# Attention and a SiLU projection pair on one core: q, k and v loaded over all 128 partitions in one transfer, attention output on four quarter-array tiles

## The chip, the cores and the metric

The kernel runs on one core of a Trainium2 chip. The metric is the device time of one execution in microseconds (us), on the slowest core, which here is the only one. Each kernel was executed several times. "Fast" and "slow" are the states that the runs were given by their time and clock. The profile is one execution, traced. In it PE is TensorE's matmuls, PEld its weight loads, DVE is VectorE, ACT ScalarE, POOL GpSimd and SP SyncE, which issues most transfers.

## The reference

Linear attention over 8 batches, 8 heads, 576 tokens and 64 features per head, then a two-layer projection with SiLU on the 4608 tokens.

```python
q_s = exp(q) / sum(exp(q), over features)          # max subtraction left out here
k_s = exp(k) / sum(exp(k), over the sequence)
kv  = einsum('bhsd,bhse->bhde', k_s, v)            # 64 x 64 per head
x   = einsum('bhsd,bhde->bhse', q_s, kv)           # heads side by side: [4608, 512]
h   = x @ w_in                                     # [4608, 2048]
out = (h * sigmoid(h)) @ w_out                     # [4608, 512]
```

## The kernel before

Tokens lie on partitions: of the 128 partitions, 64 hold the tokens of one head (nine tokens, `J`, per partition) and 64 those of another. The 4608 tokens go through the projections in nine chunks: mm1 (`hps`, 16 groups of 4 matmuls per chunk), tanh on ACT and a product on DVE (`GT`), mm2 (`ops`, 16 groups of 4). Attention for batch b is planned a chunk ahead, between those groups: exp of q and k on ACT, normalization on DVE and POOL, a transposing transfer of q (`qT`), `kv` on PE, and `xt`, which multiplies `qT` by kv into `XT`, the input of mm1.

The loads. One tensor of one batch comes in four transfers of 288 KB, and each fills 64 partitions:

```python
def load(b, name, src, ccs=(0, 1), engs=(nc.sync, nc.sync)):
    ...
    x = src[b].rearrange("(c r g) (p j) d -> c r p g (j d)", r=2, g=2, j=J)
    for cc in ccs:
        for r in range(2):
            engs[r].dma_start(
                out=st[b][name][r * P:(r + 1) * P, 2 * cc:2 * cc + 2, :], in_=x[cc, r])
```

kv and xt. kv comes out per half `r` and pair `g`; it is copied into a block-diagonal 128x128 weight `kvbd` (zeroed once), so that one full-array matmul serves two heads:

```python
nc.vector.tensor_scalar_mul(                       # in kvcopy, for r, for g
    out=kvbd[b % 3][h, 2 * cc + r, g * 64:(g + 1) * 64],
    in0=kp[h, g * E1:g * E1 + D], scalar1=rz[h, g:g + 1])
...
nc.tensor.matmul(                                  # in xt(t, c), c = 0..3
    out=o1[:, a - first:a - first + n],
    lhsT=kvbd[b % 3][:, c, :],
    rhs=st[b]["qT"][:, col // P:(col + n) // P, cc, r * P:(r + 1) * P])
```

The start. Batch 0's loads go first, q and the first part of k from two issuing engines (SP and ACT), the rest from SP. The weights (`W1`, `W2`, fp32 in memory and cast to bf16 on the way) are issued by POOL once the first half of v is there. Batch 1's loads wait for a part of W2:

```python
nc.gpsimd.tensor_copy(gate[:, 0:1], st[0]["vt"][0:1, 1, 0:1])
load_w1(0); load_w1(1); load_w2(0); load_w1(2); load_w2(1); load_w1(3); load_w2(2); load_w2(3)
st[1]["qt"] = ld.tile(...)
nc.gpsimd.tensor_copy(st[1]["qt"][0:1, 0, 0:1], W2[0:1, 4, 0:1])   # gate of batch 1
for name, src in (("qt", q), ("kt", k), ("vt", v)):
    load(1, name, src)
```

## Time and profile before

| what | before |
|---|---|
| median of the first 3 runs | 316.25 us (316.21 to 318.23) |
| the traced run | 312.93 us, span 311.2 us |
| PE busy | 286.4 us, 92% of the span |
| steady chunk (512 tokens) | 30.43 us |
| first projection matmul starts | 21.90 us |

The page's view in 40 equal slices (7.8 us each) of the kernel before. Digits are busy tenths, PEclk is the granted clock in tenths, the last row is what the DMA engines moved.

```profile
PE   8559985889689999999999999999999999999992
...
PEclk9979999899979999999999999999999999999998
DMA  7999999999999898289838974500450050014005
GB/s 179 259 208 207 246 250 256 236 271 278 258 242 254 185 251 199 65 177 238 189 85 177 243 166 100 112 2 0 101 113 0 2 126 10 0 36 102 0 0 135
```

Read it from left to right and count the slices from 0: up to slice 11 the DMA engines are full (9, but for the first slice) and PE falls to 5 or 6 in four slices. From slice 12 PE is full, and the load of the DMA engines sinks, to 2 in slice 16 and to 0 in slice 26. The kernel has a DMA-bound stage and a TensorE-bound stage, and the average of 92% hides the first.

The chain of work that ended last, of the kernel before, as shares of the span:

```profile
PE 65%; DMA 24%; DVE 5%; POOL 1%; ACT 1%; SPq 1%; issue 1%; DVEq 0%
PE ops L231 32%; PE hps L196 30%; DMA vt<-in_v_dram 9%; DMA W_59<-in_moe_w_out_dram 5%; DMA qt<-in_q_dram 5%; DMA qT<-eq 5%; DVE zq L99 2%; PE kvps L145 1%; DVE GT L212 1%; ACT sg L204 1%; POOL W_58 L276 1%; DVE kvbd_62 L160 1%; SPq L74 1%; DMA out_dram<-ost 1%; DVE kvbd_63 L160 1%
```

A quarter of this chain is transfers: of v, W2, q and qT. The table by stretches of the kernel before shows the rates. Its columns are the stretch, its length, busy time of PE, PEld, DVE, ACT and POOL, then granted clock, DMA share and GB/s. The DMA share is the time that all packets took, as a share of the 16 engines' time; it passes 1 in these tables.

```profile
core 0: us, PE busy (x) PEld busy (x) DVE busy (x) ACT busy (x) POOL busy (x), PEclk, DMA share, GB/s
4.00:7.00 3.00, 3.00 (x12) 1.23 (x11) 0.00 (x0) 1.16 (x1) 0.00 (x0) 1.00 1.06 244
20.00:28.00 8.00, 7.69 (x52) 4.89 (x51) 6.58 (x22) 5.28 (x14) 0.00 (x0) 0.86 1.24 206
36.00:48.00 12.00, 10.99 (x72) 6.84 (x71) 7.27 (x19) 7.39 (x14) 4.23 (x2) 1.00 1.08 258
60.00:68.00 8.00, 6.70 (x33) 3.13 (x33) 5.81 (x13) 6.35 (x11) 1.50 (x1) 1.00 1.01 268
```

The first and the last row are loads of q, k and v: 244 and 268 GB/s with the engines' share at 1, so the DMA engines had no time to spare. The second row is the weight stage. Its 206 GB/s are bf16 written; twice that is read, since the weights are fp32 in memory. And these are what PE waited for, in the list of waits of the kernel before (us in total, times, longest):

```profile
PE kvps L145 <- ACT vaug_60 L90: 4.9, 2, 2.8
PE o_1020 L178 <- DMA qT<-eq: 3.8, 1, 3.8
PE kvps L145 <- DVE GT L212: 3.0, 1, 3.0
```

kv of batch 0 waits for v (4.9 us), kv of batch 1 for a DVE queue whose head waits for v (3.0), xt of batch 2 for qT (3.8). In the steady stage the timeline of PE shows what one xt costs. Columns: start, length, engine, line, operation; the length that the profile gives a group (1.03 us) is more than the distance to the next start (0.86), so the distance between starts is taken as the cost.

```profile
144.35 1.03 PE L196 MATMUL hps<-XT,W_58 128*128 128x512 bf16 x4
145.21 0.27 PE L178 MATMUL o_1631<-qT,kvbd_62 128*128 128x256 bf16 x1
145.32 0.27 PE L178 MATMUL o_1631<-qT,kvbd_63 128*128 128x256 bf16 x1
145.43 1.03 PE L231 MATMUL ops<-W_59,GT 128*128 128x512 bf16 x4
146.38 1.04 PE L196 MATMUL hps<-XT,W_58 128*128 128x512 bf16 x4
```

From 145.21 to 145.43 is one xt: 0.22 us, four times per chunk.

### The profile page before, as it was taken

How to read it: one execution, taken by the hardware profiler on the slowest of the kernel's cores; microseconds unless marked ns; L12 is line 12 of the kernel's file. 1: busy time of each engine (PE TensorE's matmuls, PEld its weight loads, DVE VectorE, ACT ScalarE, POOL GpSimd, SP SyncE). 2: the span in 40 equal slices, each digit the busy share in tenths (PEclk: the TensorE clock that was granted, in tenths of full speed). 3: DMA queues.
4: the chain of work that ended last, by engine and by line, in shares of the span. 5: the costliest groups of instructions: out<-in, count | busy, mean ns of one | idle time of the engine just before them, and what ended most of it. 6: DMA issues, size and time to landing. Idle time of an engine off the chain costs nothing.

```text
span 311.2 us, 4432 instructions
## 1 busy us (share of the span) xinstructions
PE 286.4 (92%) x1618; PEld 137.6 (44%) x1618; DVE 166.2 (53%) x342; ACT 152.4 (49%) x250; POOL 50.0 (16%) x42
## 2 busy tenths in 40 slices
PE   8559985889689999999999999999999999999992
PEld 3327653344344444444444444444444444444440
DVE  2867574476714494459355935583554454345331
ACT  3547463397354556545644655465534443543330
POOL 0520040036600043005300620071000000000000
PEclk9979999899979999999999999999999999999998
DMA  7999999999999898289838974500450050014005
GB/s 179 259 208 207 246 250 256 236 271 278 258 242 254 185 251 199 65 177 238 189 85 177 243 166 100 112 2 0 101 113 0 2 126 10 0 36 102 0 0 135
DMA packets 40183, 46.36 MB, mean 149 GB/s; under 512 B 19169, under 2 KB 23265, under 8 KB 40161
## 3 DMA queue, kind: packets, MB, share of 16 engines
q1 hardware_dynamic: 35504, 41.00, 55.9%
q0 software_dynamic: 4224, 4.19, 8.1%
q10 hardware_dynamic: 432, 0.88, 1.1%
q8 instruction: 12, 0.20, 0.3%
q14 instruction: 11, 0.08, 0.1%
HBM read 36.70 MB, written 9.44 MB: 148 GB/s over the span
## 4 chain that ended last, share of the span: by engine, by line
PE 65%; DMA 24%; DVE 5%; POOL 1%; ACT 1%; SPq 1%; issue 1%; DVEq 0%
PE ops L231 32%; PE hps L196 30%; DMA vt<-in_v_dram 9%; DMA W_59<-in_moe_w_out_dram 5%; DMA qt<-in_q_dram 5%; DMA qT<-eq 5%; DVE zq L99 2%; PE kvps L145 1%; DVE GT L212 1%; ACT sg L204 1%; POOL W_58 L276 1%; DVE kvbd_62 L160 1%; SPq L74 1%; DMA out_dram<-ost 1%; DVE kvbd_63 L160 1%
## 5 line engine op out<-in xcount | busy, mean ns | idle before, releaser
L212 DVE SCALAR_TENSOR_TENSOR GT<-sg,hps 128x512 bf16<-128x512 f32 (+2 forms) x176 | 99.7, 587 | 114.3 <-ACT sg L204 113.4
L196 PE MATMUL hps<-XT,W_58 128*128 128x512 bf16 (+3 forms) x640 | 148.1, 359 | 2.1 <-DVE GT L212 1.8
L231 PE MATMUL ops<-W_59,GT 128*128 128x512 bf16 x576 | 148.4, 382 | 0.0
L204 ACT ACTIVATE sg<-hps 128x512 f32<-128x512 f32 (+3 forms) x160 | 87.5, 554 | 119.9 <-PE hps L196 104.1
L196 PEld LDWEIGHTS <-W_58 128*128 128x128 bf16 x640 | 62.6, 98 | 68.6 <-issue 4.2
L231 PEld LDWEIGHTS <-GT 128*128 128x128 bf16 x576 | 55.0, 98 | 63.8 <-issue 4.8
L105 POOL TENSOR_TENSOR eq<-eq,rzq 128x1152 bf16<-128x1152 bf16 x14 | 29.6, 2117 | 137.6 <-ACT sg L204 95.6
L99 DVE TENSOR_REDUCE zq<-eq 128x18 f32<-128x1152 bf16 x16 | 21.6, 1348 | 6.3 <-ACT eq L85 6.3
L85 ACT ACTIVATE eq<-qt 128x1152 bf16<-128x1152 f32 x16 | 18.5, 1157 | 7.5 <-DMA qt<-in_q_dram 7.5
L85 ACT ACTIVATE ek<-kt 128x1152 bf16<-128x1152 f32 x16 | 18.7, 1168 | 2.5 <-DMA kt<-in_k_dram 2.5
L145 PEld LDWEIGHTS <-ek 64*128 64x128 bf16 x288 | 9.5, 98 | 16.9 <-issue 8.1
L244 DVE TENSOR_SCALAR ost<-ops 128x512 f32<-128x512 f32 x18 | 12.3, 686 | 6.7 <-PE ops L231 6.7
L246 ACT ACTIVATE ost<-ops 128x512 f32<-128x512 f32 x18 | 10.8, 597 | 10.2 <-PE ops L231 10.2
L145 PE MATMUL kvps<-vaug_60,ek 64*128 64x130 bf16 x144 | 6.5, 225 | 5.4 <-ACT vaug_60 L90 4.9
L305 PE MATMUL wps<-warm 128*128 128x512 bf16 x32 | 9.5, 453 | 1.2 <-DVE warm L256 1.2
L145 PE MATMUL kvps<-vaug_61,ek 64*128 64x130 bf16 x144 | 6.7, 228 | 3.5 <-DVE GT L212 3.0
L157 DVE RECIPROCAL rz<-kvps 128x2 f32<-128x2 f32 x32 | 4.9, 154 | 4.2 <-PE kvps L145 3.7
L160 DVE TENSOR_SCALAR kvbd_63<-kvps,rz 64x64 bf16<-64x64 f32 x24 | 6.8, 283 | 0.6
L160 DVE TENSOR_SCALAR kvbd_62<-kvps,rz 64x64 bf16<-64x64 f32 x24 | 6.8, 283 | 0.6
L92 POOL CAST vaug_60<-vt 128x1152 bf16<-128x1152 f32 x6 | 6.8, 1158 | 0.0
L92 POOL CAST vaug_61<-vt 128x1152 bf16<-128x1152 f32 x6 | 6.8, 1157 | 0.0
L305 PEld LDWEIGHTS <-warm 128*128 128x128 bf16 x32 | 3.5, 114 | 5.7 <-issue 2.6
(135 smaller groups left out, 78.6 us busy)
## 6 DMA issues: line engine op xcount, KB each, us to landing
vt<-in_v_dram SPq DMA_DIRECT2D x32, 288.0 KB, 9.0
out_dram<-ost SPq DMA_DIRECT2D x72, 128.0 KB, 2.4
kt<-in_k_dram SPq DMA_DIRECT2D x31, 288.0 KB, 7.9
qt<-in_q_dram SPq DMA_DIRECT2D x30, 288.0 KB, 5.8
W_58<-in_moe_w_in_dram POOLq DMA_DIRECT2D x4, 512.0 KB, 11.8
W_59<-in_moe_w_out_dram POOLq DMA_DIRECT2D x4, 512.0 KB, 18.1
qt<-in_q_dram ACTq DMA_DIRECT2D x2, 288.0 KB, 6.0
kt<-in_k_dram ACTq DMA_DIRECT2D x1, 288.0 KB, 8.4
```

Source lines behind the costliest of these rows:

```text
L85: nc.scalar.activation(out=o, in_=jgd(st[b][src], cc), func=ACT.Exp)
L92: eng.tensor_copy(o, jgd(st[b]["vt"], cc))
L99: nc.vector.reduce_sum(out=st[b]["zq"][:, cc], in_=e, axis=AX.X)
L105: eng.tensor_tensor(out=e, in0=e, in1=r[:, :, :, None].to_broadcast([128, J, 2, D]), op=ALU.mult)
L145: nc.tensor.matmul(out=t[r][:, 0:2 * E1], lhsT=st[b]["ek"][r * P:(r + 1) * P, j, cc * 128:(cc + 1) * 128], rhs=vaug[b % 2][r * P:(r + 1) * ...
L160: nc.vector.tensor_scalar_mul(out=kvbd[b % 3][h, 2 * cc + r, g * 64:(g + 1) * 64], in0=kp[h, g * E1:g * E1 + D], scalar1=rz[h, g:g + 1],)
L196: nc.tensor.matmul(out=hps[:, 0:size], lhsT=W1[:, c, fb * 128:(fb + 1) * 128], rhs=XT[t][:, c, off:off + size], start=(c == 0), stop=(c == ...
L204: nc.scalar.activation(out=sg[:, 0:size], in_=hps[:, 0:size], func=ACT.Tanh, scale=0.5)
L212: nc.vector.scalar_tensor_tensor(out=GT[g][:, fb, col:col + n], in0=sg[:, h], scalar=1.0, in1=hps[:, h], op0=ALU.add, op1=ALU.mult,)
L231: nc.tensor.matmul(out=OP[t, tb], lhsT=GT[t][:, fc, tb * 128:(tb + 1) * 128], rhs=W2[:, fc, :], start=(fc == 0), stop=(fc == NFB - 1),)
L244: nc.vector.tensor_scalar_mul(out=ost, in0=OP[t, tb], scalar1=0.5)
L305: nc.tensor.matmul(out=wps, lhsT=warm[:, 0:128], rhs=warm, start=True, stop=True)
```

## The change

Its intent: fill all 128 partitions with one transfer per tensor and batch, where each filled 64 before; and use the 64x64 structure of kv, with four independent quarter-array tiles in place of block-diagonal weights that are half zeros. The loads now put heads 2g and 2g+1 on the two halves, and the tile (row half g, column half r) writes each head to the half where the next weights expect it, so `w_in` keeps its order.

```diff
-    def load(b, name, src, ccs=(0, 1), engs=(nc.sync, nc.sync)):
+    def load(b, name, src, ccs=None):
...
-        x = src[b].rearrange("(c r g) (p j) d -> c r p g (j d)", r=2, g=2, j=J)
-        for cc in ccs:
-            for r in range(2):
-                engs[r].dma_start(
-                    out=st[b][name][r * P:(r + 1) * P, 2 * cc:2 * cc + 2, :], in_=x[cc, r]
-                )
+        x = src[b].rearrange("(g r) (p j) d -> g (r p) (j d)", r=2, j=J).rearrange("g x y -> x g y")
+        c = slice(0, NG) if ccs is None else slice(2 * ccs, 2 * ccs + 2)
+        nc.sync.dma_start(out=st[b][name][:, c, :], in_=x[:, c, :])
...
-                    out=kvbd[b % 3][h, 2 * cc + r, g * 64:(g + 1) * 64],
+                    out=kvn[b % 3][h, cc, r, :],
...
-    def xt(t, c, tags=("ring", "ring"), dve=0):
+    def xt(t, cc, tags=("ring", "ring"), dve=0):
...
-                nc.tensor.matmul(
-                    out=o1[:, a - first:a - first + n],
-                    lhsT=kvbd[b % 3][:, c, :],
-                    rhs=st[b]["qT"][:, col // P:(col + n) // P, cc, r * P:(r + 1) * P],
-                )
+                for g in range(2):
+                    for r in range(2):
+                        h = slice(g * 64, (g + 1) * 64)
+                        nc.tensor.matmul(
+                            out=o1[g][r * 64:(r + 1) * 64, a - first:a - first + n],
+                            lhsT=kvn[b % 3][h, cc, r, :],
+                            rhs=st[b]["qT"][h, col // P:(col + n) // P, cc, r * P:(r + 1) * P],
+                        )
...
-    for t in kvbd:
-        nc.vector.memset(t, 0.0)
```

Batch 0's q, k and v still come in two transfers each (one per column pair `cc`), all from SP. The places of kv and xt in the plan move by a unit or two, because xt now comes in two groups instead of four.

More of the change, by code (lines that the diff above doesn't have):

```diff
@@ L51 @@
     vaug = [glob.tile([128, J, NG * E1], BF16, name=f"vaug{i}") for i in range(2)]
-    kvbd = [glob.tile([128, NC, 128], BF16, name=f"kvbd{i}") for i in range(3)]
+    kvn = [glob.tile([128, 2, 2, D], BF16, name=f"kvn{i}") for i in range(3)]
     ident_f = glob.tile([128, 128], FP32, name="ident_f")
@@ L166 @@
     XT = {}
-    def xt(t, c, tags=("ring", "ring"), dve=0):
+    def xt(t, cc, tags=("ring", "ring"), dve=0):
         if t not in XT:
             XT[t] = mp.tile([128, NC, S], BF16, name="XT")
-        cc, r = divmod(c, 2)
         for i, (off, size) in enumerate(part[t]):
-            o1 = ps.tile([128, TCH], FP32, name="o1", tag=tags[i], bufs=PSB[tags[i]])
+            o1 = [
+                ps.tile([128, TCH], FP32, name="o1", tag=tags[i], bufs=PSB[tags[i]])
+                for _ in range(2)
+            ]
             a = first = cut[t] + off
@@ L177, in xt @@
                 n = min(S - col, first + size - a)
-                nc.tensor.matmul(
-                    out=o1[:, a - first:a - first + n],
-                    lhsT=kvbd[b % 3][:, c, :],
-                    rhs=st[b]["qT"][:, col // P:(col + n) // P, cc, r * P:(r + 1) * P],
-                )
-                a += n
-            x = XT[t][:, c, off:off + size]
-            if i < dve:
-                nc.vector.tensor_copy(x, o1[:, 0:size])
-            else:
-                nc.scalar.copy(out=x, in_=o1[:, 0:size])
+                for g in range(2):
[6 more added lines that the diff above has]
+                        )
+                a += n
+            for g in range(2):
+                x = XT[t][:, 2 * cc + g, off:off + size]
+                if g < dve:
+                    nc.vector.tensor_copy(x, o1[g][:, 0:size])
+                else:
+                    nc.scalar.copy(out=x, in_=o1[g][:, 0:size])
     GT = {}
@@ L258 @@
     make_identity(nc, ident_f)
-    both = (nc.sync, nc.scalar)
     for cc in range(2):
-        load(0, "qt", q, (cc,), both)
-    load(0, "kt", k, (0,), both)
-    load(0, "vt", v, (0,))
-    load(0, "kt", k, (1,))
-    load(0, "vt", v, (1,))
+        load(0, "qt", q, cc)
+    for cc in range(2):
+        load(0, "kt", k, cc)
+        load(0, "vt", v, cc)
     nc.vector.tensor_copy(ident, ident_f)
@@ L327 @@
     kvcopy(0, 1)
-    for c in range(NC):
-        xt(0, c, ("ring", "ops"), 1)
+    for cc in range(2):
+        xt(0, cc, ("ring", "ops"), 1)
     LAG = 6
@@ L369, in plan_attn @@
             plan(u + ks[cc] + 1, lambda cc=cc: kvcopy(b, cc))
-        for c in range(NC):
-            plan(u + ox[c], lambda c=c: xt(b, c))
+        for cc in range(2):
+            plan(u + ox[cc], lambda cc=cc: xt(b, cc))
     V = nc.vector
     plan(begin[1] - 8, lambda: load(2, "qt", q))
-    plan_attn(1, begin[1], (-16, -14, -10, -9), -7, (-4, -3), (-3, -2, -1, 0), (nc.gpsimd, nc.gpsimd), V)
-    plan_attn(2, begin[2], (-27, -24, -20, -16), -14, (-9, -7), (-5, -4, -3, -2))
+    plan_attn(1, begin[1], (-16, -14, -10, -9), -7, (-4, -3), (-2, 0), (nc.gpsimd, nc.gpsimd), V)
+    plan_attn(2, begin[2], (-27, -24, -20, -16), -14, (-10, -7), (-5, -3))
     for b in range(3, B):
-        plan_attn(b, begin[b], (-48, -44, -40, -36), -22, (-15, -11), (-9, -7, -5, -3))
-    for c in range(NC):
-        plan(begin[NCH - 1] - 9 + 2 * c, lambda c=c: xt(NCH - 1, c))
+        plan_attn(b, begin[b], (-48, -44, -40, -36), -22, (-15, -11), (-7, -4))
+    for cc in range(2):
+        plan(begin[NCH - 1] - 7 + 3 * cc, lambda cc=cc: xt(NCH - 1, cc))
     for u, (_, f) in enumerate(units):
```

## The prediction

The recorded text has passages cut where no trace or run of this case shows what they say; the cuts are marked. No term of the sum is cut: -3, -10 and +2 us were summed to -11 to -12 us of 316.25, and 304.5 us was predicted. What is gone is the reason given for the speed of full-height loads and the one given for a cost of xt above its array time, and with it one of the four cases that would have made it wrong; the author's estimates then stand on the 240 to 280 and 412 GB/s of the trace, and on kv, which takes 0.71 us where 0.49 was worked out.

> **What bounds the kernel.** From about 88 us on TensorE does: in the table by stretches it is busy 30.2 of 30.4 us per chunk of 512 tokens. A chunk costs 30.43 us: 128 matmuls of 0.216 us (27.65), kv (timeline: 0.71 + 1.11 us) and xt (four times 0.22 us). Before 88 us the kernel waits for DMA: the chain of waits runs through qt, vt, W2 and qT transfers almost without a break up to 86 us. TensorE starts its first projection at 21.9 us, then stands: 1.0 us at 44.3, 3.0 at 50 (kv, behind v's cast), 1.3 at 57 to 60, 0.8 at 66, 3.8 at 82.5 (qT of batch 2), plus some 3 us of low granted clock after these gaps: about 13 us.
>
> **The loads.** In the table by stretches the half-height loads move 240 to 280 GB/s at a DMA share of 1.05: saturated. In the weight stage (18 to 32 us), whose transfers span 128 partitions, 206 GB/s of bf16 are written, from twice the bytes read: 412 GB/s.[...] My estimate for full height is 350 to 400 GB/s: 1.18 MB in about 3.2 us, not 4.6. Four issues of 0.6 us become one, so SyncE is less held up[...] (it issued stores late, at 74 to 81.5 us, and batch 2's transpose after them).
>
> Estimate: batch 0's last v lands at 14 to 15 us, not 17.5; first projection at 18 to 19 us (gain 3). Weights start near 9 us, not 11.5; the gate on W2 that opens batch 1's loads fires near 26, not 30.4; v of batch 1 lands near 43, not 51.8, before TensorE wants it; both transposes land in time. I expect 10 of the 13 us back.
>
> **xt.** Per chunk, four full-array matmuls of 512 columns (0.87 us) become two groups of four 64x64 tiles. If four run at once, array time is 0.43 us[...]. kv, already row-tiled,[...] 18 matmuls of 130 columns, two at once, need 0.49 us and take 0.71.[...] Estimate 0.5 to 0.6 us per group: 1.1 us per chunk, +0.2 us times 9, 2 us lost. ACT's copies stay the same but come in pairs (1.16 us); the four ring buffers should cover that. The kvbd clears were hidden.
>
> **Sum.** -3 (start) -10 (gaps, clock) +2 (xt) = -11 to -12 us of 316.25: **304.5 us**, eight in ten 298 to 311. Faster by over 2%: 0.84; within 2%: 0.14; slower: 0.02.
>
> **What would show it.** First projection near 18.5 us; load stretches at 350 GB/s or more; no TensorE gap above 1.5 us between 44 and 88 us; the chain of waits leaving DMA for TensorE before 50 us; granted clock 1.0 from 30 us; steady chunks of 30.4 to 30.8 us, xt groups of 0.5 to 0.6 us.
>
> **What would make it wrong.** Full-height loads no faster than 280 GB/s: only issue time is won, about 312 us. Quarter tiles running one after another: 0.86 us per group, +8 us.[...] Or the weights setting the start.

## The result

The kernel after takes 302.36 us (302.00 to 303.06, 4 runs) beside 316.97 us before (316.21 to 318.23, 4 runs). The ratio is 0.954, 95% interval 0.950 to 0.958: faster, by 4.6%. A ratio is the mean time of one kernel's fast runs over that of the other's in the same rounds, so it is not quite the ratio of the medians quoted here. The result is correct.

The view in 40 slices of the kernel after (7.5 us each):

```profile
PE   8689939989999999999999999999999999999991
...
PEclk9999989999999999999999999999999999999998
DMA  7899999998938921794179417101720140023006
GB/s 263 239 195 203 273 391 225 395 393 197 398 92 173 364 102 39 169 332 155 35 166 334 155 35 155 30 1 29 153 41 2 30 109 2 0 49 91 2 0 139
```

TensorE is full from slice 9 on, about 68 us, where it was slice 12, about 93 us, before. There is one deep hole left, the 3 in slice 5. Load rates that were near 250 reach 391 to 398 in the best slices. The chain that ended last, of the kernel after:

```profile
PE 73%; DMA 11%; DVE 9%; ACT 2%; POOL 1%; issue 1%; SPq 0%; DVEq 0%; ACTq 0%
```

DMA's share of it fell from 24% to 11%. In order of time, its last wait for a transfer ends at 39.2 us (86 before). The same stretches as before, of the kernel after, in the same columns:

```profile
4.00:7.00 3.00, 3.00 (x12) 1.24 (x11) 1.44 (x2) 2.33 (x2) 0.00 (x0) 1.00 1.02 354
20.00:28.00 8.00, 8.00 (x59) 5.65 (x58) 5.58 (x19) 5.03 (x14) 0.00 (x0) 1.00 1.23 200
36.00:48.00 12.00, 7.15 (x36) 3.96 (x35) 7.46 (x15) 7.05 (x12) 4.24 (x2) 0.86 0.98 346
60.00:68.00 8.00, 7.18 (x37) 3.42 (x36) 6.29 (x11) 6.27 (x9) 5.77 (x4) 1.00 1.05 393
```

The loads went from 244 to 354 and from 268 to 393 GB/s at the same share of the engines' time. The weight stage did not change. But in the third row PE is busy 7.15 of 12 us, less than before (10.99), and at a clock of 0.86. That is a new wait, and the timeline of the kernel after around it shows how it comes about (PE lines, then ACT lines):

```profile
36.65 1.03 PE L235 MATMUL ops<-W_59,GT 128*128 128x512 bf16 x4
42.52 1.92 PE L200 MATMUL hps<-XT,W_58 128*128 128x320 bf16 x8 [4.85 <-DVE GT L216]
...
39.28 1.16 ACT L83 ACTIVATE eq<-qt 128x1152 bf16<-128x1152 f32 x1 [5.73 <-DMA qt<-in_q_dram]
40.35 0.69 ACT L208 ACTIVATE sg<-hps 128x320 f32<-128x320 f32 x2
```

The trace shows ACT working in order. The exp of batch 1's q stands in its queue ahead of chunk 0's tanh (`sg`), and that q was issued at 28.35 us and landed at 39.2 us, beside the last weights on full DMA engines (share 1.24 to 1.25 from 28 to 32 us). So ACT stood 5.73 us, its tanh came late, the buffers of mm1 stayed taken, and PE stood 4.85 us; its clock then fell (eight matmuls in 1.92 us at 42.52, where they take 1.14 at full clock). Before, PE reached this place 4.5 us later, and q had come in two parts.

The steady stage. The second xt group of a chunk in the timeline of PE, kernel after:

```profile
138.79 1.03 PE L235 MATMUL ops<-W_59,GT 128*128 128x512 bf16 x4
139.75 0.30 PE L181 MATMUL o_1639<-qT,kvn_62 64*64 64x256 bf16 x2
139.75 0.30 PE L181 MATMUL o_1640<-qT,kvn_62 64*64 64x256 bf16 x2
139.88 0.27 PE L181 MATMUL o_1639<-qT,kvn_63 64*64 64x256 bf16 x2
139.89 0.27 PE L181 MATMUL o_1640<-qT,kvn_63 64*64 64x256 bf16 x2
140.09 1.04 PE L200 MATMUL hps<-XT,W_58 128*128 128x512 bf16 x4
```

Four matmuls start together at 139.75 and four at 139.88: the quarter tiles do run four at once. The group before ends at 139.65 (138.79 plus four times 0.216), so this one costs 0.44 us; the chunk's first group, whose pairs start 0.17 us apart, costs 0.59. Together 1.03 us per chunk, beside four times 0.22 plus 0.09 us of pause, 0.97, before. So it is in four of the six chunks after kv of batch 3; in the last two both groups start together and cost 0.44 each. Worked out from 0.216 us for 512 columns, the array time was halved (0.87 to 0.43 us per chunk, four tiles at once). The pauses took it back: in the group above 0.10 us pass from the end of mm2 (139.65) to the first tiles, then 0.13 to the next tiles and 0.21 to mm1 (140.09), where 256 columns take 0.108.

Where the time came from, by starts of the same work in the timelines (us). The last two columns are the second traces of both kernels (e8 and e7 below):

| start of | before | after | before again | after again |
|---|---|---|---|---|
| first projection of chunk 0 | 21.90 | 17.41 | 22.25 | 17.20 |
| kv of batch 1 | 53.06 | 50.69 | 54.07 | 50.67 |
| kv of batch 2 | 77.43 | 71.45 | 78.71 | 71.43 |
| kv of batch 3 | 107.85 | 97.02 | 111.20 | 96.99 |
| last run of mm2 | 300.02 | 289.85 | 303.36 | 289.83 |

All the gain is there by kv of batch 3: 10.8 us in the first pair of traces and 14.2 in the second. After it the kernel after takes 0.7 us more (192.83 from there to the last mm2, against 192.17). Some 0.3 of that is one wait of kv for a copy by DVE (0.44 us at 132 us, where the kernel before waits 0.17); e3 below has the tiles without that wait and takes 192.56. The tile groups themselves cost about 0.4 us.

### The profile page after: what moved, and what is told of

It is laid out like the page before. It is cut to its first block, busy times and chain, and to the rows that moved or that the text cites. A ratio compares the mean times of both kernels' runs of the same rounds, so it can differ in the third digit from the quotient of the medians.

```text
span 301.3 us, 4439 instructions
## 1 busy us (share of the span) xinstructions
PE 283.7 (94%) x1682; PEld 133.4 (44%) x1682; DVE 165.4 (55%) x339; ACT 152.8 (51%) x250; POOL 50.9 (17%) x42
## 4 chain that ended last, share of the span: by engine, by line
PE 73%; DMA 11%; DVE 9%; ACT 2%; POOL 1%; issue 1%; SPq 0%; DVEq 0%; ACTq 0%
PE ops L235 36%; PE hps L200 33%; DMA W_59<-in_moe_w_out_dram 4%; DMA qt<-in_q_dram 4%; DVE zq L97 3%; DMA vt<-in_v_dram 3%; DVE GT L216 2%; PE kvps L143 2%; ACT sg L208 1%; POOL W_58 L276 1%; DVE kvn_62 L158 1%; DVE rzq L98 1%; DVE kvn_64 L158 1%; ACT eq L83 1%; SPq L74 0%
## 5 line engine op out<-in xcount | busy, mean ns | idle before, releaser
L143 PEld LDWEIGHTS <-ek 64*128 64x128 bf16 x288 | 8.8, 93 | 10.7 <-issue 5.1
L143 PE MATMUL kvps<-vaug_60,ek 64*128 64x130 bf16 x144 | 6.2, 217 | 3.0 <-ACT vaug_60 L88 2.2
L143 PE MATMUL kvps<-vaug_61,ek 64*128 64x130 bf16 x144 | 5.9, 217 | 0.3 <-DVE kvn_64 L158 0.2
```

Of the source, the lines that this page charges most:

```text
L143: nc.tensor.matmul(out=t[r][:, 0:2 * E1], lhsT=st[b]["ek"][r * P:(r + 1) * P, j, cc * 128:(cc + 1) * 128], rhs=vaug[b % 2][r * P:(r + 1) * ...
```

## The experiments

The theory, S: the gain is that of the loads, because a transfer that reaches only partitions 0 to 63, or only 64 to 127, moves fewer GB/s than one that reaches both sides of partition 64. Rivals: B, fewer issues on SyncE; C, the quarter tiles; H, a 64-row transfer is slow for its height and not for where it lies. The expectations of e1 to e3 call the theory of the loads A, because sides and height are not told apart there; e9 and e10 do that.

### e1: the loads alone

The kernel before with the `load` of the kernel after and its first loads. xt keeps the full array and `kvbd`, so the heads are in a wrong order and the result is wrong; shapes and waits are those of a right one. The edit in words:

```diff
 # kernel before
-    load as before, first loads from two engines
+    load as after, first loads as after
```

> The kernel before with the full-height loads alone; xt stays four full-array matmuls with block-diagonal weights, so heads sit in a wrong order and the result is wrong on purpose (every shape and wait is as it would be). Theory A (the height of the loads carries the gain): 300.5 to 302.5 us, as fast as the whole change or up to 1.5 us faster[...]; first projection near 17.5 us. Theory C (the quarter tiles carry a good part of it, through fewer array columns and no kvbd): 306 us or more.

Measured: 301.92 us (300.33 to 303.54, 6 runs), ratio 0.953 (0.949 to 0.957). That is the whole gain, without the tiles. From kv of batch 3 to the last mm2 it takes 192.17 us, exactly as before, where the kernel after takes 192.83: so the tiles, with the plan that was moved for them, cost 0.7 us over the steady stage and give nothing. C is out as the source of the gain. The wait of mm1 is there too, so it belongs to the loads; from the list of waits of e1:

```profile
PE hps L193 <- DVE GT L209: 5.4, 2, 4.6
```

### e2 and e3: four transfers per load, half height or full height

Both are the kernel after with each load in four transfers of 288 KB, as many as before. e2 takes half-height ones, with the heads placed as in the kernel after; e3 takes one transfer per column group over all 128 partitions.

```diff
 # e2, in load (first loads: q and the first k from two engines, as before)
+        x = src[b].rearrange("(c g r) (p j) d -> c r p g (j d)", r=2, g=2, j=J)
+        for cc in ccs:
+            for r in range(2):
+                engs[r].dma_start(
+                    out=st[b][name][r * P:(r + 1) * P, 2 * cc:2 * cc + 2, :], in_=x[cc, r])
 # e3, in load
-        nc.sync.dma_start(out=st[b][name][:, c, :], in_=x[:, c, :])
+        for g in range(NG)[c]:
+            nc.sync.dma_start(out=st[b][name][:, g:g + 1, :], in_=x[:, g:g + 1, :])
```

> The kernel after, with each load split again into half-height transfers as before (two halves times two column pairs, 288 KB each, the first ones from two engines), heads placed as after, so the result is right. Theory A (height) and theory B (fewer issues) both say that the gain of the loads is gone: 315 to 318 us, the loads at 240 to 280 GB/s again. Theory C: 305 to 309 us.

> The kernel after, with each load cut into four transfers of 288 KB that all span 128 partitions: as many issues as before, full height. Theory A (height): 301 to 304 us, load stretches still at 350 to 400 GB/s. Theory B (the number of issues on SyncE): 312 to 317 us, as with the half-height split.

Measured: e2 317.21 us (315.64 to 318.09, 6 runs), ratio 1.000 (0.997 to 1.004): nothing of the gain is left, with the tiles and all else of the change in place. e3 299.10 us (297.98 to 300.44, 6 runs), ratio 0.943 (0.939 to 0.948). The stretch 60 to 68 us in the tables by stretches, first of e2, then of e3:

```profile
60.00:68.00 8.00, 6.97 (x37) 3.06 (x36) 5.57 (x12) 6.72 (x12) 1.57 (x1) 1.00 1.04 243
```

```profile
60.00:68.00 8.00, 7.95 (x40) 3.82 (x40) 5.38 (x8) 6.71 (x10) 5.01 (x4) 1.00 1.05 391
```

The same number of transfers of the same size, and 243 against 391 GB/s. The issue count, B, is out; the height of the transfer is what matters. e3 was expected to equal the kernel after. It beat it by about 1%, which no theory had said; e5 takes that up. And not every stretch of e3 was as fast: from 4 to 7 us it moved 300 GB/s at a DMA share of 0.95, where the kernel after moved 354. Why is open.

### e9 and e10: what about the height?

Both are the kernel after with each load cut by rows into a 64-row and two 32-row transfers, in the same order; batch 0's three 64-row transfers go first. Only the place of the rows differs; in memory, too, both 64-row transfers read one unbroken stretch per pair of heads.

```diff
+    PARTS = ((32, 96), (0, 32), (96, 128))     # e9;  e10: ((0, 64), (64, 96), (96, 128))
...
-        nc.sync.dma_start(out=st[b][name][:, c, :], in_=x[:, c, :])
+        for lo, hi in parts:
+            nc.sync.dma_start(out=st[b][name][lo:hi, c, :], in_=x[lo:hi, c, :])
...
+    for part_ in (PARTS[:1], PARTS[1:]):
+        for name, src in (("qt", q), ("kt", k), ("vt", v)):
+            load(0, name, src, None, part_)
```

> The kernel after with every load cut by rows: partitions 32 to 95 in one transfer, then 0 to 31, then 96 to 127; of batch 0 the three 64-row transfers (q, k, v, 590 KB each) go first, so from 3 to 7 us nothing else moves. Theory S ([...]what counts is that a transfer reaches partitions on both sides of 64[...]): these 64-row transfers run as fast as full-height ones, 330 to 360 GB/s from 3 to 7 us. Rival H (a transfer of 64 rows is slow for its height, wherever it lies): 235 to 265 GB/s, as in the kernel before. The 32-row transfers reach one side only and are slow under both, so the whole time is of less interest: 304 to 312 us under S, 315 us or more under H.

> The control: the same three transfers per load, of the same sizes in the same order, but the 64 rows are partitions 0 to 63 and the 32 rows are 64 to 95 and 96 to 127. Both theories expect 235 to 265 GB/s or less from 3 to 7 us[...]. Under S this kernel is slower than the one with rows 32 to 95, by 3 us or more; under H the two agree within 1 us.

The stretch 4 to 7 us, in which only the 64-row transfers move, in the tables by stretches, first of e9 (rows 32 to 95), then of e10 (rows 0 to 63):

```profile
4.00:7.00 3.00, 3.00 (x12) 1.20 (x11) 0.00 (x0) 0.00 (x0) 0.00 (x0) 1.00 1.02 383
```

```profile
4.00:7.00 3.00, 3.00 (x10) 1.09 (x9) 0.00 (x0) 0.00 (x0) 0.00 (x0) 1.00 1.06 214
```

A 64-row transfer across the middle moves 383 GB/s, as much as a full-height one (354 in this stretch of the kernel after, 393 from 60 to 68 us); the same transfer on partitions 0 to 63 moves 214. H is out. It is not the height but which partitions a transfer reaches, as S had said. What in the hardware makes the difference, and whether the border lies exactly at partition 64, these runs do not show.

The whole times: e9 317.11 us (4 runs, ratio 1.002, 0.999 to 1.005), e10 323.03 us (4 runs, ratio 1.021, 1.018 to 1.025). S had expected e9 at 304 to 312 us and missed: once the 32-row transfers run, which reach one side each, e9 moves 228 GB/s (8 to 14 us), and PE waits 7.6 us for the normalized q of batch 0. The difference between the two, 5.9 us, is on the side of S, which had said 3 us or more.

### e4: q of batch 1 let go earlier

```diff
-    st[1]["qt"] = ld.tile([128, NG, J * D], FP32, name="qt")
-    nc.gpsimd.tensor_copy(st[1]["qt"][0:1, 0, 0:1], W2[0:1, 4, 0:1])
+    for name, fc in (("qt", 0), ("kt", 4)):
+        st[1][name] = ld.tile([128, NG, J * D], FP32, name=name)
+        nc.gpsimd.tensor_copy(st[1][name][0:1, 0, 0:1], W2[0:1, fc, 0:1])
```

> The kernel after, with q of batch 1 let go when the first quarter of W2 has landed and not the second; k and v of batch 1 keep the gate on the second quarter. In the kernel after, TensorE stands 4.9 us at 37 to 42 us and then runs at a low clock, because ScalarE waits in order for q of batch 1 (landed at 39.2 us) before the tanh of chunk 0. If that is the cause: q lands near 30 to 33 us, the gap falls below 1 us, and the time drops by 4 to 6 us to 296 to 298 us. If the weights come too late in exchange[...], the gap moves to a projection waiting for weights and the time stays near 302 us.

Measured: 300.09 us (299.49 to 301.62, 4 runs), ratio 0.948 (0.943 to 0.952): faster than the kernel after by 2.3 us, not by 4 to 6. The two were not run in the same rounds, and their ratios overlap (0.950 to 0.958 for the kernel after), but none of their times do (302.00 at least there). The first exp of batch 1's q starts at 33.0 us and the wait at 37 us is gone, as expected. In its place the list of waits of e4 has two others, the longest of 2.0 and 1.0 us:

```profile
PE kvps L143 <- DVE GT L216: 2.2, 2, 2.0
...
PE ops L235 <- DMA W<-in_moe_w_out_dram: 1.0, 1, 1.0
```

The weights come late in exchange (1.0 us), and PE, now earlier, waits 2.0 us at kv of batch 1, behind DVE's queue, in which the cast of batch 1's v stands.

### e5: q of batch 1 in two transfers

One edit in the kernel after, full height kept:

```diff
-    for name, src in (("qt", q), ("kt", k), ("vt", v)):
+    for cc in range(2):
+        load(1, "qt", q, cc)
+    for name, src in (("kt", k), ("vt", v)):
         load(1, name, src)
```

> The kernel after with one edit: q of batch 1 comes as two full-height transfers (one per column pair, 576 KB) instead of one of 1152 KB. The run with every load cut in four was about 1% faster than the kernel after. Theory P: that 1% is q of batch 1 alone: one transfer has one completion, so the first exp waits for all of it while ScalarE holds back the tanh of chunk 0; with two, the first exp starts near 36.5 us instead of 39.3, and the time is 299 to 300 us, 2 to 4 us under the kernel after. Rival Q: finer pieces help all over (exps, casts and frees of every batch start earlier): then this edit gives less than 1 us and 301.5 to 302.5 us come out.

Measured: 299.02 us (298.33 to 300.75, 6 runs), against 302.64 for the kernel after on the same chip (e7). Theory P holds: this edit alone gives the 3.6 us, as much as cutting every load in four. The timeline of e5, one line of ACT and one of PE:

```profile
34.44 1.16 ACT L83 ACTIVATE eq<-qt 128x1152 bf16<-128x1152 f32 x1 [1.33 <-DMA qt<-in_q_dram]
...
41.57 1.14 PE L200 MATMUL hps<-XT,W 128*128 128x320 bf16 x8 [1.88 <-DVE GT L216]
```

The first exp starts 4.8 us earlier than in the kernel after (4.1 earlier than in e7, where it starts at 38.58; 36.5 had been expected), and ACT does tanhs between the two halves. PE's longest wait there falls from 4.85 to 1.88 us, and its next groups run at full clock (1.14 us for eight matmuls, where the kernel after needed 1.92). This is the fastest kernel together with e3, and it beats both kernels.

### e6: e3 and e4 together

> Both edits that were faster together: all loads in four full-height transfers, and q of batch 1 let go one weight quarter earlier. If the two remove different waits (the wait for q at 37 us; the wait for v's cast at 44 us): 296 to 298 us. If both remove the same wait: 298.5 to 300 us, as each of them alone.

The edits are those of e3 and e4. Measured: 299.63 us (298.51 to 301.62, 6 runs): no faster than e3 or e5 alone, so 296 to 298 was missed and the second case came out. From the list of waits of e6:

```profile
PE ops L236 <- DMA W<-in_moe_w_out_dram: 1.9, 1, 1.9
PE kvps L144 <- DVE GT L217: 1.6, 2, 1.4
```

The wait for q is gone and two waits for other transfers have come, the second through DVE's queue, in which the cast of v waited 4.8 us for its transfer. In e4, e5 and e6 kv of batch 1 starts at 46.8, 46.3 and 47.8 us. This is consistent with all of them being held by the same thing, the transfers that must be in before it: letting q go first delays W2 and v by as much. Which order of these transfers is best was not tried further.

### e7 and e8: both kernels again

> The kernel after, unchanged, beside the others on the same chip: 301.5 to 303 us, ratio to the kernel before 0.952 to 0.956; the gap of 4 to 5 us at 37 to 42 us is there again in the profile.

> The kernel before, unchanged, for a second trace. Its first profiled execution took 312.9 us, while its timed ones take 315.5 to 319.2. If the trace on record was a lucky one, this one spans 313 to 317 us, and the missing 3 to 4 us are in the DMA-bound stage: the wait for qT of batch 2 near 82 us is 6 us or more instead of 3.8, and the steady chunks are still 30.4 us.

e7: 302.64 us (301.91 to 303.04, 6 runs), the same wait again. Its ratio, 0.958 (0.954 to 0.962), is higher than the first 0.954, and than the 0.952 to 0.956 expected, although its median is nearly the same. In this call one execution of the kernel before took only 312.77 us, and by that three of its eleven executions, at 317.7 to 318.2, were called slow and left out; in the call of e1 to e4 the same kernel's times up to 319.2 counted as fast. The medians before are alike (316.60 and 316.75).

e8: 316.27 us (one run, so of unknown state), span 314.5, against 311.2 in the trace on record. Two of PE's waits in its list of waits:

```profile
PE o L178 <- DMA qT<-eq: 5.8, 2, 5.4
...
PE kvps L145 <- DVE GT L212: 4.0, 1, 4.0
```

They were 3.8 and 3.0 us in the first trace (for qT, 6 or more had been expected, and 5.4 came). kv of batch 3 starts at 111.20 us and not 107.85, and from there on both traces take the same time (192.16 and 192.17). So the trace was a lucky execution of the kernel before: its timed runs lie near the second trace, and one of 11 was as short.

## Why the prediction was right, and where its terms were off

The time, 302.4 us, lies in the range of 298 to 311 and near the 304.5 predicted. Point by point:

- **Two stages, DMA-bound up to 88 us.** Right, and shown: e2 takes only the full-height loads away, and all the gain goes.
- **Loads at 350 to 400 GB/s.** Right: 354 to 393. That it is the place of the rows and not their number is shown by e9 and e10 (383 and 214 GB/s); why the place counts is not shown.
- **Start 3 us earlier.** Too small: 4.5 us in the first pair of traces, 5.0 in the second. The last cast of v started at 13.3 us, where the prediction had 14 to 15 for v. The weights did not start near 9 but at 11.5 us, as before (10.3 in the second trace); they did not set the start.
- **10 of 13 us of gaps and cold clock won.** The 13 us were read from one trace, and that was a fast one: its span was 3.3 us shorter than e8's, all of it in this stage. Net of the start, the traces won 6.3 us (10.8 minus 4.5) and the second pair 9.2 (14.2 minus 5.0).
- **No gap after 44 us, clock at 1.0 from 30 us.** Half wrong. The waits for v and qT did go, but a new gap of 4.85 us opened at 37.7 us, and the clock was 0.86 from 36 to 48 us. The step that failed is the estimate of batch 1's loads. It timed v alone (43 us, before kv wants it), and that nearly held: the cast of v began at 45.9 us, and kv did not wait for it. It gave no time for q, whose exp stands in ACT's queue ahead of chunk 0's tanh. The gate fired at 28.2 us (27.3 in the second trace), not 26, and q then took 10.9 us from issue to landing, beside the last weights. The prediction also did not see that one transfer has one completion: the first exp, which needs half of q, now waits for all of it (it starts at 39.28 us, and at 34.44 with two transfers, e5). e5 measures that at 3.6 us.
- **xt costs 2 us.** The new cost was right: four tiles at once, a pause before each group, 0.44 and 0.59 us per group where 0.5 to 0.6 was estimated. The difference was mis-sized, because the old cost was 0.97 us in most chunks and not 0.87, and the last two chunks had no slow group: the groups cost about 0.4 us over the steady stage, 0.7 with the one wait for DVE, instead of 2. What a group costs above its array time, 0.216 us with four tiles at once, was the estimate from kv; its cause was not shown: 0.10 us passes between the end of mm2's last matmul (139.65) and the first tile (139.75), but the kernel before has a pause of 0.09 us between mm2 and mm1 (before 146.38), where both are full-array matmuls.
- **Weight loads of xt.** The 64-column loads of `kvn` take 104 ns on average, as long as the 128-column ones of `kvbd` did before (102 to 107). Four of the small ones ran within 0.11 us, side by side (170.27), so no cost of them is seen.
- **The sum.** -3, -10 and +2 were -11 to -12 us; 14.6 us was measured. The start was worth more, the tiles cost less, and the base was slower than the trace that the sum was built on. The new gap took back some of it. That 304.5 came within 2.2 us of the measured time is in part luck: a loss of 3.6 us that was not foreseen (e5) stood against a larger gain at the start, a slower base and cheaper tiles.

Left open: why in four chunks the tiles of the first group start 0.17 us apart, while those of the second, and both groups of the last two chunks, start together.

## What to carry to other kernels

When a kernel has a stage that waits for transfers at a full DMA share, look at which partitions each transfer reaches, not at how many transfers there are: 243 and 391 GB/s came from as many transfers of the same size (e2, e3), 214 and 383 from transfers of 64 rows each in different places (e10, e9). Then cut the transfer at the point where its first consumer can start, because the first exp of batch 1's q, which needs half of it, waited for the whole transfer (39.28 us, and 34.44 with two), and ACT, which worked in order, stood 5.73 us before it with chunk 0's tanh behind. And take the losses that a sum is built on from more than one trace when the timed runs scatter by 1%.

## Further measurements

- Alternating halves: loads in half-height transfers, one half after the other, moved 240 to 268 GB/s (kernel before in both traces, e2; 4 to 7 and 60 to 68 us), beside 214 for rows 0 to 63 alone (e10, 4 to 7 us), 12% to 25% more.
- Size at full height: at a DMA share of 1.05 (60 to 68 us), transfers of 288 KB moved 391 GB/s (e3) and those of 1152 KB 393 (kernel after); only at the start (4 to 7 us) were the small ones slower, 300 beside 354 with 576 KB. The kernel with the larger ones took about 3.5 us longer (302.64 beside 299.10 for e3); for q of batch 1 e5 shows why.
- One copy on POOL: in the trace after, its copy of one element, the gate of the weights, took 1.13 us. It began at 10.43 us, inside a DVE product of two SBUF operands (10.16 to 11.52), and ended about with it (11.56). In the trace before it took 0.18 us (at 11.33), between two such products (8.72 to 10.08 and from 11.79). Two traces do not prove the cause.
